# Attention with normed q and k, then an MLP: squares and sums by head, a k copy in two parts, one MLP copy on VectorE

## The chip, the cores and the metric

The kernel runs on one core of a Trainium2 chip. The metric is device time in microseconds (us) of one execution. Engines: TensorE (PE; its weight loads are PEld), VectorE (DVE), ScalarE (ACT), GpSimd (POOL) and SyncE (SP), which issues DMAs. Each engine runs its own instructions in order; semaphores order them across engines. Each kernel has several timed runs and one profiled execution.

## What is computed

q, k and v have the shape (8, 12, 448, 64): batches, heads, sequence, head dimension. Cut to what matters:

```python
def rmsnorm(x, g):
    return x / np.sqrt(np.mean(x * x, axis=-1, keepdims=True) + 1e-6) * g
q_n, k_n = rmsnorm(q, g_q), rmsnorm(k, g_k)
scores = np.matmul(q_n, k_n.transpose(0, 1, 3, 2)) / np.sqrt(64)
attn = softmax(scores)
x = np.matmul(attn, v)                 # then (3584, 768): heads side by side
h = x @ w_in                           # (3584, 2048)
g = np.maximum(h, 0) + alpha * np.minimum(h, 0)
out = g @ w_out                        # (3584, 768), float32
```

## The kernel before

**Tiling.** The 12 heads of a batch are taken four at a time, so there are 3 groups per batch and 24 groups in all, numbered y. A group's q (or k) is one tile `nat` of 128 partitions by 2 heads, 7 sequence parts and 64 values: 64 partitions for one half of the heads and 64 for the other, with 2 heads of each half beside each other. Its 448 keys are 7 key tiles j of 64.

**A group's preparation.** `load_qk` loads q and k. `square` writes squares in float32 to `sq` (line 148, GpSimd; q of group 1 on ScalarE). `reduce` sums them over the 64 values to `ss` (line 154, VectorE, one instruction of 128 x 896 for q and one for k). `root` takes logarithm and exponential on ScalarE (lines 165 and 166) to get the reciprocal root `rr`. `scale` multiplies `nat` by `rr` to `qs` in float16 (line 171; VectorE for groups 0 to 2 and q of group 3, GpSimd from then on). TensorE transposes the 7 parts into PSUM (`tps`), and VectorE copies these to SBUF as `qT` and `kT`, multiplying k by the gains. Group 0 does it in parts of its own (`part_...`), group 1 in `turn_one` (q: line 256, k: line 258), groups 2 to 6 in `turn` (lines 298 and 300), later groups by a transposing DMA. `follow` is a tiny GpSimd copy `mark` (line 244) that holds GpSimd back until VectorE's scaling is done.

**Attention.** `score(y, j)` makes the scores of one key tile (line 315) in one of two PSUM buffers `sc`; `soft` takes the exponential on ScalarE into `expT` (line 329). `den` and `attv` sum the exponentials and multiply them by v (line 344); `log` and `invert` (lines 361 and 366) give the reciprocal of the sums, with which VectorE writes `xT` (lines 393 and 395).

**MLP.** `up(b, ft)` makes one of 16 blocks `hT` of h for a batch (line 410). The MLP copy `ah` = alpha times h is ScalarE's (line 447); of ft = 2 and 3 of the first batch it is VectorE's (line 441), whose maxima are put off until ft = 4. `tensor_max` on VectorE writes `gT` (line 449). `down` multiplies by w_out (line 459), copies to `osb` (line 471) and stores (line 479).

**Order.** It is written by hand. The 168 key tiles are cut into bursts n (0: tiles 0 and 1 of group 0, 3: tile 6 of group 0 and tile 0 of group 1, 4: tiles 1 and 2 of group 1, and so on). `bursts`, `dens`, `avs`, `turns` and `gaps` say what stands in each burst; `post` (filled by `after`) holds what is appended behind a burst, `mid[1] = 1` and `mid[4] = 2` put a group's root and scaling ahead of the burst's last exponential. `reduce` of group 2 stands behind burst 3, that of group 3 (G = 3) behind a later burst, `square` two bursts before it. `spin` makes matrix products on idle data between the first bursts (line 488).

```python
    def root(y, nms="qk"):
        ...
        nc.scalar.activation(out=rr, in_=ss, func=AF.Ln, scale=1.0 / D, bias=epsb[:, 0:1])
        nc.scalar.activation(out=rr, in_=rr, func=AF.Exp, scale=-0.5)
```

Of the kernel before, what the change touches and what calls it, by code (L numbers as in the profile page):

```python
# [11 lines left out]
AF = mybir.ActivationFunctionType  # L12
ALU = mybir.AluOpType
AXIS_X = mybir.AxisListType.X
# [7 lines left out]
def kernel(  # L22
# [12 lines left out]
    nc = tc.nc  # L35

    B, H, S, D = q.shape
    DM = H * D
    DF = moe_w_in.shape[1]
    J = S // 64  # L40
    HH = H // 2
    G = HH // 2
    KM = DM // 128
    NF = DF // 128
# [39 lines left out]
    alpha_sb = cols[:, :NF]  # L84
    gain = cst.tile([128, 1], FP32, name="gain", tag="gain")
# [7 lines left out]
    nat, sqs, qs, ss_t, rr_t, qkT, vt, xT = {}, {}, {}, {}, {}, {}, {}, {}  # L93
# [47 lines left out]
    def square(y, nm):  # L141
        src = nat[y, nm].rearrange("p h j d -> p (h j d)")
        sq = ld.tile([128, 2 * J, D], FP32, name="sq", tag="sq", bufs=4)
        sqf = sq.rearrange("p n d -> p (n d)")
        if (y, nm) == (1, "q"):
            nc.scalar.activation(out=sqf, in_=src, func=AF.Square)
        else:
            nc.gpsimd.tensor_mul(out=sqf, in0=src, in1=src)  # L148
        sqs[y, nm] = sq

    def reduce(y, nm):
        if nm == "q":
            ss_t[y] = ld.tile([128, 2, 2, J], FP32, name="ss", tag="ss", bufs=4)
        nc.vector.tensor_reduce(  # L154
            out=ss_t[y][:, "qk".index(nm)].rearrange("p h j -> p (h j)").unsqueeze(2),
            in_=sqs[y, nm], axis=AXIS_X, op=ALU.add,
        )

    def root(y, nms="qk"):
        n = len(nms)  # L160
# [85 lines left out]
    def turn_one(y, nm):  # L246
        t = psf.tile([128, 512], FP32, name="tps", tag="mm")
        tp = t[:, :S].bitcast(FP16).rearrange("p (j c) -> p j c", j=J)
        for j in range(J):
            nc.tensor.transpose(  # L250
                tp[:, j, :], qs[y, nm][:, j].rearrange("p h d -> p (h d)"), ident
            )
        t = att.tile([128, J, 2, 64], FP16, name=f"{nm}T", tag=f"{nm}T", bufs=4)
        o = t.rearrange("p j g c -> p j (g c)")
        if nm == "q":
            nc.vector.tensor_copy(out=o, in_=tp)
        else:
            nc.vector.tensor_scalar(
                out=o, in0=tp, scalar1=gain[:, 0:1], scalar2=None, op0=ALU.mult
            )  # L260
        qkT[y, nm] = t

    def turn_dma(y):
# [134 lines left out]
    def bank(name, spare):  # L398
        if spare:
            t = psa.tile([128, 2, 512], FP32, name=name + "a", tag="acc")  # L400
            return t[:, 0]
        return psf.tile([128, 512], FP32, name=name, tag="mm")
# [3 lines left out]
    def up_part(hT, b, ft, lo, hi):  # L406

        for i in range(lo, hi):
            for g in range(2):
                nc.tensor.matmul(  # L410
                    out=hT[:, :S],
                    lhsT=w_in_sb[:, g * G + i, ts(ft, 128)],
                    rhs=xT[b][:, g, i, :],
                    start=(i == 0 and g == 0),
                    stop=(i == G - 1 and g == 1),
                )
# [10 lines left out]
    held = []  # L427

    def up(b, ft, spare=False):
        if b == 0 and ft in begun:  # L430
            hT = begun[ft]

            for n in {2: (2, 3), 3: ()}.get(ft, (ft,)):
                up_part(begun[n], 0, n, G - 1, G)
        else:
            hT = bank("hT", spare)
            up_part(hT, b, ft, 0, G)
        ah = ffn.tile([128, S], FP16, name="ah", tag="ah", bufs=3)
        if b == 0 and ft in (2, 3):

            nc.vector.tensor_scalar(
                out=ah, in0=hT[:, :S], scalar1=alpha_sb[:, ft : ft + 1], scalar2=None,
                op0=ALU.mult,
            )
            held.append((hT, ah, ft))
            return
        nc.scalar.activation(out=ah, in_=hT[:, :S], func=AF.Copy, scale=alpha_sb[:, ft : ft + 1])  # L447
        for hT, ah, ft in [(hT, ah, ft)] + (held if b == 0 and ft == 4 else []):
            nc.vector.tensor_max(out=gT[:, ft, ds((b & 1) * S, S)], in0=hT[:, :S], in1=ah)  # L449

# [52 lines left out]
    while m < NG * J or steps:  # L503
        n = len(bursts)
# [20 lines left out]
        while len(bursts[n]) < limit and m < NG * J:  # L525
            y, j = divmod(m, J)
# [13 lines left out]
    def at(n, f, *a):  # L540
        prep.setdefault(max(int(n), 0), []).append((f, a))

    def after(n, f, *a):
        post.setdefault(max(int(n), 0), []).append((f, a))
# [9 lines left out]
    for y in range(G, NG):  # L554

        early = y < G + 2
        if early:
            n = turn_at[y - 1] + 1
        elif y == G + 2:
            n = den_at[G - 1]  # L560
        elif y == 2 * G:
            n = turn_at[y] - 4
        elif y % G == 1:
            n = den_at[y - 4] - 1
        elif y % G:
            n = den_at[y - G]
        else:
            n = av_at[y - 4]
        if y in (3 * G - 1, 3 * G):

            after(den_at[G] - (y < 3 * G), load_qk, y)
        else:
            at(n - (6 if early else 3 if y == 2 * G else 4 if y < 3 * G else 5), load_qk, y)
        for nm in "qk":
            if y != 2 * G:
                after(n - 2, square, y, nm)
            if early:
                after(n, reduce, y, nm)
            else:
                jobs.setdefault(n + (y == G + 2 and nm == "k"), []).append((reduce, (y, nm)))  # L580
        if y == 3 * G:
            after(n, *jobs[n].pop()[:1], y, "k")
        roots[n + 1 + (y in (G + 2, 3 * G))] = y
# [7 lines left out]
    for b in range(B):  # L591
        ups = [(UP / 3 if b == 0 and ft < 4 else UP, up, (b, ft)) for ft in range(NF)]
        odd = b % 2
        new = [
            (DOWN, down, (b - odd, t, oh))
            for t in (range(3, J) if odd else range(3)) for oh in range(2)
        ]
        if b == 0:
            new.sort(key=lambda u: u[2][2])
        tail = len(new) if b == B - 1 else 4 if b == 0 else 2 if odd else 1  # L600
        periods.append((ups, carry, new[:tail]))
        carry = new[tail:]
# [65 lines left out]
    for n, g in enumerate((g_q, g_k)):  # L668
        for h in range(2):
            nc.gpsimd.dma_start(  # L670
                out=rows[NF + n : NF + n + 1, ds(64 * h, 64)], in_=g.unsqueeze(0)
# [12 lines left out]
    for h in range(2):  # L684
# [8 lines left out]
    part_scale("k", lo, K0, nc.vector)  # L693
    part_root("k", hi)
    square(1, "q")
    nc.vector.tensor_copy(out=cols, in_=ct[:, : NF + 2])
    nc.vector.tensor_mul(
        out=gain, in0=cols[:, NF : NF + 1], in1=cols[:, NF + 1 : NF + 2]
# [6 lines left out]
    part_scale("k", hi, J - K0, nc.vector)  # L705
    follow(0, "k")
    square(1, "k")
    reduce(1, "q")
    square(2, "q")
    after(0, part_turn, "k", range(K0, J))  # L710
    after(0, part_copy, "k", hi, nc.vector)
    after(0, reduce, 1, "k")
    mid[1] = 1
    after(1, square, 2, "k")
    after(1, load_w_in, 0)
    for nm in "qk":
        after(3, reduce, 2, nm)
    after(5, load_w_in, 1)
    after(7, load_w_in, 2)
    after(8, load_w_in, 3)  # L720
# [7 lines left out]
    for n in range(NB):  # L728
# [6 lines left out]
        for t in first_tiles:  # L735
            if t == (0, J - 2):
                spin(1)
            elif t == (1, J - 3):
                spin(2, False)
            elif t == (1, J - 2):  # L740
                spin(1, False)
            elif t == (0, J - 1):
                turn_one(1, "q")
            elif t == (1, 0):
                turn_one(1, "k")
            elif t == (1, J - 1):
                turn(2)
            score(*t)
            if n == den_at[G - 1] - 1 and t == tiles[-1]:
                begin(0)  # L750
                begin(1)
            elif lead and t == tiles[0]:
                soft(*t)
                den(dens[n])
                attv(avs[n], 0, True, (log, invert))
            elif lead and t == tiles[1]:
                begin(2)
# [28 lines left out]
        if n in roots:  # L786
            y = roots[n]
# [41 lines left out]
        for k, (f, a) in enumerate(gaps[n]):  # L829
# [3 lines left out]
            else:  # L833
                f(*a, spare)
                done += 1
                if n in jobs and not (lead and done < 5):
                    g, c = jobs[n].pop(0)
# [3 lines left out]
                while late and done == late[0][0]:  # L841
                    _, g, c = late.pop(0)
# [43 lines left out]
```

## Time and profile before

| | |
|---|---|
| median of 6 runs | 430.32 us (429.41 to 431.14) |
| profiled execution's own time | 429.86 us |
| its span, first to last instruction | 427.7 us |
| mean granted TensorE clock | 0.995 |
| busy: PE, ACT, DVE, POOL | 97%, 65%, 49%, 40% |
| exponentials, line 329 | 168 of 1003 ns |
| reductions, line 154 | 46 of 1076 ns |
| GpSimd squares, line 148 | 45 of 1681 ns |

Times in the profile count from the span's start. The page shows busy time, the span in 40 slices, DMA queues, the chain of work that ended last, and the costliest groups of instructions. The timeline lists one engine's instructions by time; where like instructions follow each other they are one row, with their count behind an x. In brackets stands the time the engine sat idle before a row, and what ended it. "By stretches" gives the busy time in chosen stretches, the clock granted to TensorE (1.00 is full speed) and the DMA engines' share.

### The profile page before, as it was taken

The numbers are of one execution on the slowest core, as the hardware profiler recorded it, in microseconds if no ns is written. First come the engines' busy times: TensorE is split into PE (matmuls) and PEld (weight loads), VectorE is DVE, ScalarE is ACT, GpSimd is POOL, SyncE is SP. The second block draws the span as 40 slices with busy tenths as digits, with TensorE's granted clock in tenths as the row PEclk, the third lists the DMA queues.
The fourth block names the chain that finished last, engine by engine and source line by source line (L and its number), as shares of the span: only waits on it lengthen the run. The fifth ranks groups of instructions, "written<-read, shape, count | busy, mean of one in ns | idle before, by whom it ended". The sixth has DMA issues, their size and how long they took to land.

```text
span 427.7 us, 11526 instructions
## 1 busy us (share of the span) xinstructions
PE 416.6 (97%) x4975; PEld 216.9 (51%) x4975; DVE 207.9 (49%) x314; ACT 276.5 (65%) x385; POOL 172.5 (40%) x135
## 2 busy tenths in 40 slices
PE   8799999999999999999999999999999999999996
PEld 3334445544455555554555445544555445555564
DVE  4865954456544454545345463545453453243421
ACT  5898888778875685768576676767666577132200
POOL 6679994475467209360465408380253000000000
PEclk9989999999999999999999999999999999999999
DMA  8999999999389804986278823863083201211033
GB/s 203 255 234 189 194 202 209 195 188 227 66 147 162 220 12 83 193 152 141 41 120 189 190 67 80 171 138 95 21 149 74 62 1 21 57 38 37 20 74 76
DMA packets 68531, 53.39 MB, mean 125 GB/s; under 512 B 35568, under 2 KB 68480, under 8 KB 68480
## 3 DMA queue, kind: packets, MB, share of 16 engines
q1 hardware_dynamic: 53680, 39.73, 42.1%
q0 software_dynamic: 13984, 11.81, 18.9%
q10 hardware_dynamic: 816, 1.11, 1.0%
q8 instruction: 39, 0.64, 0.6%
q14 instruction: 12, 0.10, 0.1%
HBM read 45.62 MB, written 11.01 MB: 132 GB/s over the span
## 4 chain that ended last, share of the span: by engine, by line
PE 90%; ACT 5%; DVE 2%; POOL 1%; issue 1%; ACTq 1%; POOLq 0%
PE op L459 29%; PE hT L410 22%; PE hTa L410 11%; PE sc L315 8%; PE opa L459 6%; PE dn L344 5%; PE av L344 5%; ACT expT L329 3%; PE avb L344 2%; DVE osb L471 1%; ACTq L105 1%; PE tps L291 1%; PE spin L488 1%; PE hTb L410 1%; ACT ah L447 0%
## 5 line engine op out<-in xcount | busy, mean ns | idle before, releaser
L329 ACT ACTIVATE expT<-sc,expb 128x896 f16<-128x896 f32 x168 | 161.5, 1003 | 36.9 <-PE sc L315 36.1
L171 POOL TENSOR_TENSOR qs<-nat,rr 128x896 f16<-128x896 f32 x41 | 70.0, 1728 | 139.6 <-issue 93.2
L459 PE MATMUL op<-w_out_sb,gT 128*128 128x384 f16 (+1 forms) x752 | 126.3, 323 | 0.0
L459 PEld LDWEIGHTS <-gT 128*128 128x128 f16 x912 | 85.8, 98 | 64.6 <-issue 12.0
L410 PEld LDWEIGHTS <-w_in_sb 128*128 128x128 f16 x768 | 73.3, 98 | 72.4 <-issue 7.7
L410 PE MATMUL hT<-xT,w_in_sb 128*128 128x448 f16 x510 | 106.6, 353 | 0.0
L447 ACT ACTIVATE ah<-hT,cols 128x448 f16<-128x448 f32 x85 | 53.7, 633 | 45.2 <-PE hT L410 45.1
L148 POOL TENSOR_TENSOR sq<-nat 128x896 f32<-128x896 f32 x45 | 74.7, 1681 | 7.4 <-DMA nat<-in_q_dram 4.1
L449 DVE TENSOR_TENSOR gT<-hT,ah 128x448 f16<-128x448 f32 x85 | 52.8, 623 | 49.0 <-ACT ah L447 49.0
L471 DVE COPY osb<-op 128x384 f32<-128x384 f32 (+1 forms) x47 | 25.7, 548 | 88.0 <-PE op L459 88.0
L315 PE MATMUL sc<-qT,kT 64*32 64x448 f16 (+1 forms) x1092 | 53.7, 357 | 4.7 <-ACT expT L329 2.3
L410 PE MATMUL hTa<-xT,w_in_sb 128*128 128x448 f16 x246 | 53.2, 352 | 0.0
L154 DVE TENSOR_REDUCE ss<-sq 128x14 f32<-128x896 f32 x46 | 48.4, 1076 | 0.8 <-POOL sq L148 0.8
L447 ACT ACTIVATE ah<-hTa,cols 128x448 f16<-128x448 f32 x41 | 26.0, 634 | 31.4 <-PE hTa L410 31.4
L449 DVE TENSOR_TENSOR gT<-hTa,ah 128x448 f16<-128x448 f32 x41 | 25.6, 623 | 26.7 <-ACT ah L447 26.7
L315 PEld LDWEIGHTS <-kT 64*32 64x32 f16 (+1 forms) x1092 | 15.4, 93 | 36.8 <-issue 29.8
L459 PE MATMUL opa<-w_out_sb,gT 128*128 128x384 f16 x160 | 27.7, 326 | 0.0
L395 DVE TENSOR_TENSOR xT<-av,rden 128x896 f16<-128x896 f32 x16 | 17.5, 1091 | 19.7 <-PE av L344 16.7
L344 PEld LDWEIGHTS <-vt 64*32 64x32 f16 (+1 forms) x1260 | 18.9, 94 | 13.1 <-issue 2.1
L344 PE MATMUL dn<-expT,ones 64*32 64x448 f16 (+1 forms) x812 | 24.2, 350 | 0.9
L344 PE MATMUL av<-expT,vt 64*32 64x448 f16 (+1 forms) x812 | 24.1, 349 | 0.0
L361 ACT ACTIVATE rden<-dn 128x896 f32<-128x896 f32 x16 | 14.5, 906 | 7.3 <-PE dn L344 7.3
(59 smaller groups left out, 168.2 us busy)
## 6 DMA issues: line engine op xcount, KB each, us to landing
out_dram<-osb SPq DMA_DIRECT2D x109, 96.0 KB, 2.3
nat<-in_q_dram SPq DMA_DIRECT2D x46, 224.0 KB, 4.9
nat<-in_k_dram SPq DMA_DIRECT2D x46, 224.0 KB, 5.4
vt<-in_v_dram POOLq DMA_DIRECT2D x16, 336.0 KB, 8.2
w_in_sb<-in_moe_w_in_dram POOLq DMA_DIRECT2D x12, 256.0 KB, 7.0
w_out_sb<-in_moe_w_out_dram POOLq DMA_DIRECT2D x4, 768.0 KB, 10.9
nat<-in_q_dram ACTq DMA_DIRECT2D x2, 224.0 KB, 4.4
nat<-in_k_dram ACTq DMA_DIRECT2D x2, 224.0 KB, 5.4
```

What stands on the lines that cost most here:

```text
L148: nc.gpsimd.tensor_mul(out=sqf, in0=src, in1=src)
L154: nc.vector.tensor_reduce(out=ss_t[y][:, "qk".index(nm)].rearrange("p h j -> p (h j)").unsqueeze(2), in_=sqs[y, nm], axis=AXIS_X, op=ALU.add,)
L171: eng.tensor_mul(out=t.rearrange("p j h d -> p h j d"), in0=nat[y, nm], in1=rr_t[y][:, "qk".index(nm)].unsqueeze(3).broadcast_to((128, 2, ...
L315: nc.tensor.matmul(out=sc[ds(64 * g + m * c, m), par, :S].rearrange("p (j c) -> p j c", j=J), lhsT=kT[ds(64 * par, 64), j, g, ts(c, m)], r ...
L329: nc.scalar.activation(out=expT[y][:, j], in_=scs[y, j][:, :, :S], func=AF.Exp, scale=QK_SCALE, bias=expb[:, 0:1],)
L344: nc.tensor.matmul(out=accs[g][ds(m * h, m), :S], lhsT=weights(g, y, par, ts(c, m), j), rhs=expT[y][ds(64 * g, 64), j, par, :], start=(j = ...
L395: nc.vector.tensor_mul(out=x, in0=av[:, :, :S], in1=r)
L410: nc.tensor.matmul(out=hT[:, :S], lhsT=w_in_sb[:, g * G + i, ts(ft, 128)], rhs=xT[b][:, g, i, :], start=(i == 0 and g == 0), stop=(i == G ...
L447: nc.scalar.activation(out=ah, in_=hT[:, :S], func=AF.Copy, scale=alpha_sb[:, ft : ft + 1])
L449: nc.vector.tensor_max(out=gT[:, ft, ds((b & 1) * S, S)], in0=hT[:, :S], in1=ah)
L459: nc.tensor.matmul(out=ops[c][:, :PW], lhsT=gT[:, ft, ts(t, 128)], rhs=w_out_sb[:, ft, ds(oh * OH + c * PW, PW)], start=(ft == 0), stop=(f ...
L471: nc.vector.tensor_copy(out=o[:, ts(c, PW)], in_=ops[c][:, :PW])
```

## The change

Four edits. GpSimd's squares of q of group 2 and of k of group 3 become two instructions, one for each of the tile's two heads (448 columns each). The sums of these two are taken by head too: for q of group 2 the first head's sum is appended behind burst 0 (so it stands ahead of group 1's scaling on VectorE) and the second head's stays behind burst 3; for k of group 3 both stay where the one was. `turn_one` copies k of group 1 from PSUM in two instructions, of key tiles 0 and 1 and of tiles 2 to 6. And the MLP copy of ft = 12 (NF - 4) of the first batch goes from ScalarE to VectorE, its maximum directly behind it. All else, TensorE's and SyncE's orders included, stays as it is.

```diff
@@ square
-            nc.gpsimd.tensor_mul(out=sqf, in0=src, in1=src)
+            n = 2 if (y, nm) in ((2, "q"), (G, "k")) else 1
+            for h in range(n):
+                c = ts(h, 2 * J * D // n)
+                nc.gpsimd.tensor_mul(out=sqf[:, c], in0=src[:, c], in1=src[:, c])
@@ reduce
-    def reduce(y, nm):
-        if nm == "q":
+    def reduce(y, nm, heads=None):
+        if y not in ss_t:
             ss_t[y] = ld.tile([128, 2, 2, J], FP32, name="ss", tag="ss", bufs=4)
-        nc.vector.tensor_reduce(
-            out=ss_t[y][:, "qk".index(nm)].rearrange("p h j -> p (h j)").unsqueeze(2),
-            in_=sqs[y, nm], axis=AXIS_X, op=ALU.add,
-        )
+        o = ss_t[y][:, "qk".index(nm)].rearrange("p h j -> p (h j)").unsqueeze(2)
+        for c in [slice(0, 2 * J)] if heads is None else [ts(h, J) for h in heads]:
+            nc.vector.tensor_reduce(
+                out=o[:, c], in_=sqs[y, nm][:, c], axis=AXIS_X, op=ALU.add
+            )
@@ turn_one
-            nc.vector.tensor_scalar(
-                out=o, in0=tp, scalar1=gain[:, 0:1], scalar2=None, op0=ALU.mult
-            )
+            for c in (slice(0, 2), slice(2, J)):
+                nc.vector.tensor_scalar(
+                    out=o[:, c], in0=tp[:, c], scalar1=gain[:, 0:1], scalar2=None,
+                    op0=ALU.mult,
+                )
@@ up
-        if b == 0 and ft in (2, 3):
+        if b == 0 and ft in (2, 3, NF - 4):
             nc.vector.tensor_scalar(
                 out=ah, in0=hT[:, :S], scalar1=alpha_sb[:, ft : ft + 1], scalar2=None,
                 op0=ALU.mult,
             )
-            held.append((hT, ah, ft))
-            return
-        nc.scalar.activation(out=ah, in_=hT[:, :S], func=AF.Copy, scale=alpha_sb[:, ft : ft + 1])
+            if ft < 4:
+                held.append((hT, ah, ft))
+                return
+        else:
+            nc.scalar.activation(
+                out=ah, in_=hT[:, :S], func=AF.Copy, scale=alpha_sb[:, ft : ft + 1]
+            )
@@ the order of the groups' preparation
-                after(n, reduce, y, nm)
+                after(n, reduce, y, nm, (0, 1) if (y, nm) == (G, "k") else None)
@@ the order by hand
     after(0, reduce, 1, "k")
+    after(0, reduce, 2, "q", (0,))
     mid[1] = 1
     after(1, square, 2, "k")
     after(1, load_w_in, 0)
-    for nm in "qk":
-        after(3, reduce, 2, nm)
+    after(3, reduce, 2, "q", (1,))
+    after(3, reduce, 2, "k")
```

## The prediction

> **What bounds the kernel now.** I read the page's busy shares and its chain first, then busy time by stretches, then the timelines of the first 65 us engine by engine, since every edit lies there.
>
> ```profile
> PE 416.6 (97%) x4975; PEld 216.9 (51%) x4975; DVE 207.9 (49%) x314; ACT 276.5 (65%) x385; POOL 172.5 (40%) x135
> PE 90%; ACT 5%; DVE 2%; POOL 1%; issue 1%; ACTq 1%; POOLq 0%
> ```
>
> TensorE is the bound. By stretches of 40 us it is busy 39.85 or 40.00 of 40 from 65 us on, so what the head wins by 64 us reaches the end, and nothing later gives it back. The head is another matter. Its stretches of 3.41 us (columns: stretch, its length, TensorE busy with its count, granted clock, DMA share, GB/s):
>
> ```profile
> 10.30:13.71 3.41, 2.29 (x23) 1.00 1.09 265
> 13.71:17.12 3.41, 3.28 (x27) 1.00 1.22 241
> 17.12:20.54 3.42, 1.72 (x23) 1.00 1.19 252
> 20.54:23.95 3.41, 3.41 (x16) 0.50 1.13 252
> 23.95:27.36 3.41, 2.68 (x35) 1.00 1.22 239
> ```
>
> After a stretch that is busy to 0.50 the clock is at half for 3.41 us; after one busy to 0.67 (2.29 of 3.41) it is not. The timelines of VectorE, TensorE and ScalarE there (start, length, instruction, and in brackets the idle time before it and what ended it):
>
> ```profile
> 17.30 0.62 DVE L256 COPY qT<-tps 128x896 f16<-128x896 f16 x1
> 18.04 0.68 DVE L258 TENSOR_SCALAR kT<-tps,gain 128x896 f16<-128x896 f16 x1
> 18.64 2.07 DVE L154 TENSOR_REDUCE ss<-sq 128x14 f32<-128x896 f32 x2
> 18.78 0.57 PE L315 MATMUL sc<-qT,kT 64*64 64x448 f16 x8 [0.78 <-DVE kT L258]
> 20.59 1.86 PE L488 MATMUL spin<-gT 128*128 128x448 f32 x2
> 22.38 0.59 PE L315 MATMUL sc<-qT,kT 64*64 64x448 f16 x4
> 19.21 1.90 ACT L329 ACTIVATE expT<-sc,expb 128x896 f16<-128x896 f32 x2 [0.37 <-PE sc L315]
> 23.02 1.01 ACT L329 ACTIVATE expT<-sc,expb 128x896 f16<-128x896 f32 x1 [0.54 <-PE sc L315]
> 24.27 4.70 ACT L329 ACTIVATE expT<-sc,expb 128x896 f16<-128x896 f32 x5 [0.25 <-PE sc L315]
> ```
>
> Scores of group 1 wait 0.78 for the one copy of its k (L258), then ScalarE waits 0.37 for the scores. At half clock the spin takes 1.79 until the next scores at 22.38, where the same spin at 15.07 took 0.95, and ScalarE waits again, 0.54 and 0.25. From 24.27 to 33.92 the chain is mostly ScalarE's: exponentials, root, logarithm, inverse. TensorE has it from 33.96. So the head's price is ScalarE's three waits. The last place is at 57 us:
>
> ```profile
> 57.17 0.62 ACT L447 ACTIVATE ah<-hT,cols 128x448 f16<-128x448 f32 x1
> 57.69 1.00 ACT L329 ACTIVATE expT<-sc,expb 128x896 f16<-128x896 f32 x1
> 58.74 0.38 PE L315 MATMUL sc<-qT,kT 64*64 64x448 f16 x4 [0.31 <-ACT expT L329]
> 57.83 0.62 DVE L449 TENSOR_TENSOR gT<-hT,ah 128x448 f16<-128x448 f32 x1 [1.26 <-ACT ah L447]
> ```
>
> TensorE waits 0.31 for the exponential that stands behind the MLP copy of ft = 12.
>
> **The k copy in two parts.** One instruction of 0.68 becomes two, of 256 and 640 columns. This form's rows are 0.408 (384 columns), 0.486 (512) and 0.684 (896): 0.20 + 0.54 ns a column. So 0.34 and 0.55, overlapping by 0.08 as neighbours here do. The scores of key tiles 0 and 1 read only the first part, so they start at 18.44 instead of 18.78. ScalarE's exponentials before run to 18.84, so its next starts at 18.87: 0.34 won, and the 0.37 wait is gone. The second part ends at 18.85, 0.17 later than now; its first reader, tile 2, stood at 20.27 and moves to 19.93, so 1.08 cover it. Behind it on VectorE stand group 2's reductions.
>
> **Group 2's q by head.** They would end 0.17 later (20.88) while ScalarE comes to the root 0.34 earlier (21.01 to 20.67): a wait of 0.2. So half a reduction goes ahead, into VectorE's 0.64 of idle before 15.29. It costs 0.61 (the 448-column row of L194). GpSimd's two squares run from 11.85 to 15.16; the first half of the second is there at about 14.4, VectorE is free at 14.56, ends at 15.18, and the scaling of group 1 at 15.29 is not late. Afterwards one half reduction (18.77 to 19.38) and k's, which needs the square that ends at 19.33, end at 20.43. The root finds them done with 0.24 to spare. The price is on GpSimd: a second instruction. No row shows a half square; its extra lies between nothing and 0.19 (the `mark` copy, a whole small GpSimd instruction); I take 0.05, since two full squares follow each other with 1.64 between starts at a length of 1.68. Up to 0.13 hides ahead of 15.29. Above that VectorE's scaling might wait: at 29.52 a GpSimd scaling beside VectorE's own took 2.58 instead of 1.68, so these two forms can exclude each other. At worst 0.06.
>
> The page SBUF — State Buffer of the Trainium skill (section SBUF: two separate sides) says that a VectorE instruction with two SBUF inputs and a GpSimd one exclude each other for a whole instruction. The row at 29.52 agrees.
>
> **Group 3's k by head.** GpSimd's squares at 23.99 follow VectorE's scaling, which follows the root: 0.34 earlier, so they end at about 27.0, with the first half at 26.2. If ScalarE has won 1.28 by then it wants the root at 27.58. VectorE: q's reduction 25.2 to 26.3, the first half to 26.8, the second 27.02 to 27.63: 0.07 late. Undivided it would end at 28.10, 0.5 late. With 0.54 won (below) the root is wanted at 28.32, and both forms are in time. GpSimd then issues w_in loads (27.25 to 29.42, about 0.3 earlier) before scaling group 3's k; that scaling ended at 32.10, its transposes stand at 32.97, so 0.9 cover it, and as VectorE's scaling would now be ahead of it, it needn't take 2.58.
>
> **The clock.** The stretch 17.12 to 20.54 gains 0.34 of busy time: 2.06 of 3.42, share 0.60, between 0.50 (fell) and 0.67 (held). If it still falls at 20.54: the spin starts at 20.25, does 0.29 of its 0.95 at full clock and 0.66 in 1.32, ends at 21.86, 0.52 ahead of 22.38; ScalarE's exponentials at 23.02 and 24.27 come 0.52 to 0.54 earlier. Won: 0.54. If it holds: the two gaps vanish; start to start they cost 23.02 - 21.49 - 0.91 = 0.62 and 24.27 - 23.02 - 0.91 = 0.34. Won: 0.34 + 0.96 - 0.07 = 1.23.
>
> TensorE: Matmul & The Clock Gate of the Trainium skill (section Why this matters for your kernels) says that the clock falls after an idle gap of about 3 us. Here gaps of 0.78 and 0.92 were enough, so the measurement decides; by the page there would be no fall in either kernel and the sum would be 0.34 + 0.31.
>
> **The MLP copy of ft = 12.** ScalarE loses 0.62; the exponential behind it starts at 57.17 instead of 57.69 and ends at 58.18, and the scores that waited follow those at 58.05 directly, at 58.43: 0.31 won. VectorE gains an instruction of 0.67 (L441) into an idle of 1.26: hT is done at 56.85, copy to 57.52, maximum to 58.1 instead of 58.45, so the bank is free earlier. If VectorE were not idle, 0.67 would stand before that maximum.
>
> **The sum.** Against the profiled execution's 429.86 (span 427.7 and 2.16 around it): 0.54 + 0.31 = 0.85 if the clock falls, 1.23 + 0.31 = 1.54 if it holds. The reported time is a median of executions that differ by 1.7 us among themselves before, and that median, 430.32, is 0.46 above the profiled one. Where the clock's stretches lie may differ between executions; the share 0.60 is midway between held and fallen. So I take the middle, 1.2: 429.1. What a measurement of this kernel can tell from no change is about 0.2%, 0.86 us.
>
> **The rivals.** *The clock falls as before* (against: 0.34 more busy time; for: 0.60 is near 0.50): 430.32 - 0.85 = 429.5.
> *The gain is lost in part before 34 us.* GpSimd's part wins only 0.3, and if the scaling of group 3's k takes 2.58 again from 29.2 it ends at 31.8 against transposes wanted at about 31.7; executions that never fell win only 0.34. Then 0.34 + 0.31 = 0.65 or somewhat less: 429.8.
> *Slower: the clock falls at another place.* A stretch that would now be busy to 0.50 or less between 23.95 and 30.8 costs up to half of 3.41, 1.7, where TensorE is close behind the chain: 1.7 - 0.85 = 0.85 more, 431.2. The decision point is 1.7 busy in such a stretch. Against: 23.95 to 27.36 has 2.68, and the earlier exponentials only shorten its gap of 0.60.
> *It doesn't do what it says*: were scores of tile 0 held by the second part, they would start at 18.9, and 0.17 be lost in the head. In the changed program the wait on VectorE moves to tile 2's weights, which speaks against it; I count it in the second rival.
>
> **Numbers.** Forecast 0.48, clock falls 0.32, lost in part 0.13, slower 0.07. The first is faster by over 0.86 in 0.43, the second half the time (0.16), the third hardly (0.01): faster 0.60, same 0.33, slower 0.07. The range goes from the full 1.54 with some more, 428.4, to the third case with 0.5 of scatter, 430.3.
>
> **What would show it.** After: VectorE's first k part about 0.34 long, scores of group 1 near 18.44, no ScalarE wait there; a half reduction before 15.3; clock 1.00 from 20.5 to 24 (or 0.50 and the second case); the scores near 58 us without a wait on an exponential; TensorE's first down product near 62.7 instead of 63.88. Wrong: a wait of group 1's scaling on GpSimd, a root waiting for a reduction, or a half-clock stretch elsewhere.

## The result and the profile after

| | before | after |
|---|---|---|
| median | 429.88 us (44 executions, 429.40 to 431.14) | 429.30 us (20, 428.42 to 430.38) |
| ratio, after to before | | 0.9977, 95% interval 0.9970 to 0.9985 |
| profiled execution | 429.86, span 427.7 | 429.40, span 427.6 |
| ... to the end of the last matrix product | 423.87 | 423.23 |
| ... from there to the span's end | 3.80 | 4.39 |
| ... outside the span | 2.19 | 1.78 |

Faster by 0.23%, 0.98 us between the means that the ratio compares (430.09 and 429.12). Between the two medians it is 0.58, and 1.02 from the median that the prediction started from. The forecast was 429.1. But the last three rows say that the profiled pair gets there in a way that the prediction doesn't have: the head of the program wins 0.63, the end of the program loses 0.59, and 0.41 is won outside the span.

Executions of one kernel differ by how many stretches of half clock (3.41 us each) fall into the head, which the mean granted clock tells: about 1.00 for none, 0.996 for one, 0.992 for two. Times are therefore also compared at an equal number (medians of all timed executions, us):

| | none | one | two |
|---|---|---|---|
| before | 429.45 | 429.87 | 430.77 |
| after | 428.49 | 429.36 | 430.38 (one execution) |

So at an equal number of stretches the change wins 0.96, 0.51 and 0.39 us. The mix differs too. By their times 14 of the 44 executions of before have none, 14 one and 16 two; of the 20 after, 9 have none, 10 one and 1 two. The gain at an equal number, averaged with the shares of before, is 0.57 us, with those of after 0.64. The other 0.3 to 0.4 of the 0.98 us comes from executions with two such stretches having become rare.

The page of the changed kernel, busy line and chain (before: PE 416.6, ACT x385, DVE x314, POOL x135, chain ACT 5%):

```profile
PE 415.7 (97%) x4975; PEld 217.0 (51%) x4975; DVE 209.2 (49%) x318; ACT 276.2 (65%) x384; POOL 172.0 (40%) x137
...
PE 91%; ACT 3%; DVE 2%; issue 1%; POOL 1%; ACTq 1%; POOLq 0%
```

VectorE has four instructions more, GpSimd two more, ScalarE one less. TensorE is 0.9 less "busy" with as many products; products under half clock count as longer work. ScalarE's share of the chain went from 5% to 3%.

Stretches of 3.41 us in the changed kernel (columns as before: stretch, length, TensorE busy with its count, granted clock, DMA share, GB/s):

```profile
8.67:12.08 3.41, 1.91 (x20) 1.00 1.08 239
12.08:15.49 3.41, 3.35 (x15) 0.50 1.14 227
15.49:18.90 3.41, 3.41 (x30) 1.00 1.21 205
18.90:22.32 3.42, 2.12 (x19) 1.00 1.13 251
22.32:25.73 3.41, 2.95 (x33) 1.00 1.10 228
```

The boundaries lie 1.6 us earlier against the program than in the profiled execution of before. So the clock fell at 12.08, before the edited place, and held from 20.5 to 24. This puts the whole head behind 12 us about 0.9 later than in an execution at full clock; differences between rows still read well. The edited place on TensorE and ScalarE in this execution:

```profile
19.38 0.64 PE L323 MATMUL sc<-qT,kT 64*64 64x448 f16 x8 [0.44 <-DVE kT L265]
19.82 1.91 ACT L337 ACTIVATE expT<-sc,expb 128x896 f16<-128x896 f32 x2 [0.23 <-PE sc L323]
22.09 6.47 ACT L337 ACTIVATE expT<-sc,expb 128x896 f16<-128x896 f32 x7
28.73 0.32 ACT L170 ACTIVATE rr<-ss,epsb 128x28 f32<-128x28 f32 x1 [0.17 <-DVE ss L160]
```

The scores of group 1 wait 0.44 for k instead of 0.78: the 0.34 of the prediction. Seven exponentials run without a gap where before had gaps of 0.54 and 0.25. The root of group 3 now waits 0.17 for a sum. The MLP place:

```profile
57.93 0.57 PE L323 MATMUL sc<-qT,kT 64*64 64x448 f16 x8
58.43 0.95 PE L299 MATMUL tps<-ident,qs 128*128 128x128 f16 x14
56.90 0.68 DVE L449 TENSOR_SCALAR ah<-hT,cols 128x448 f16<-128x448 f32 x1 [0.46 <-PE hT L418]
63.25 0.98 PE L472 MATMUL op<-w_out_sb,gT 128*128 128x384 f16 x5
```

Eight scores follow each other, and the transposes come 0.50 after the first of them instead of 1.01 (58.05 to 59.06). The first down product stands at 63.25 instead of 63.88. The rows of before:

```profile
58.05 0.38 PE L315 MATMUL sc<-qT,kT 64*64 64x448 f16 x4
59.06 0.95 PE L291 MATMUL tps<-ident,qs 128*128 128x128 f16 x14
63.88 2.44 PE L459 MATMUL op<-w_out_sb,gT 128*128 128x384 f16 x14
```

Then the end of the program, which the prediction took to be the same. The DMA view from shortly before the last two stores' issue (from 424 us in before, from 423.5 in after): of its queues the row of q14 (packets, MB and share of the window), then the issues with size and us from issue to landing. q14 is a queue that loads instructions. First before, then after:

```profile
q14 instruction: 1, 0.01, 0.3%
issues: line engine op xcount, KB each, median us to landing
out_dram<-osb SPq DMA_DIRECT2D x1, 48.0 KB, 1.9
out_dram<-osb ACTq DMA_DIRECT2D x1, 48.0 KB, 2.1
```

```profile
q14 instruction: 1, 0.01, 0.9%
issues: line engine op xcount, KB each, median us to landing
out_dram<-osb SPq DMA_DIRECT2D x1, 48.0 KB, 2.6
out_dram<-osb ACTq DMA_DIRECT2D x1, 48.0 KB, 2.7
```

The same two stores take 0.6 to 0.7 longer to land. In both there is one load of instructions (8192 bytes). By its start in the trace it comes at 429.29 before, 1.6 behind the span's end, and at 424.81 after, in the middle of the last stores, issued at 423.66. Where this load falls is what the last experiment turns on.

### The profile page after: what moved, and what is told of

It reads as the page before. It is cut to its first block, busy times and chain, and to the rows that moved or that the text cites. A ratio compares the mean times of both kernels' runs of the same rounds, so it can differ in the third digit from the quotient of the medians.

```text
span 427.6 us, 11531 instructions
## 1 busy us (share of the span) xinstructions
PE 415.7 (97%) x4975; PEld 217.0 (51%) x4975; DVE 209.2 (49%) x318; ACT 276.2 (65%) x384; POOL 172.0 (40%) x137
## 4 chain that ended last, share of the span: by engine, by line
PE 91%; ACT 3%; DVE 2%; issue 1%; POOL 1%; ACTq 1%; POOLq 0%
PE op L472 29%; PE hT L418 22%; PE hTa L418 11%; PE sc L323 8%; PE opa L472 6%; PE dn L352 5%; PE av L352 5%; PE avb L352 2%; ACT expT L337 2%; DVE osb L484 1%; PE spin L501 1%; POOL sq L152 1%; ACTq L105 1%; PE tps L299 1%; PE hTb L418 1%
## 5 line engine op out<-in xcount | busy, mean ns | idle before, releaser
L152 POOL TENSOR_TENSOR sq<-nat 128x896 f32<-128x896 f32 (+1 forms) x47 | 74.9, 1617 | 7.7 <-DMA nat<-in_q_dram 7.6
L160 DVE TENSOR_REDUCE ss<-sq 128x14 f32<-128x896 f32 (+1 forms) x48 | 48.7, 1037 | 1.4 <-POOL sq L152 1.2
```

What stands on the lines that cost most here:

```text
L152: nc.gpsimd.tensor_mul(out=sqf[:, c], in0=src[:, c], in1=src[:, c])
L160: nc.vector.tensor_reduce(out=o[:, c], in_=sqs[y, nm][:, c], axis=AXIS_X, op=ALU.add)
```

## The experiments

Theory: the k copy and the MLP copy win time on the path of ScalarE and TensorE in the head, the sums by head keep the roots from giving it back, and the clock adds or takes some tenths. Rivals: one of the four edits does it all; the clock does it.

**Each of the two copies alone.** The first kernel is that of before with only the two-part copy in `turn_one`, the second with only `ft in (2, 3, NF - 4)` in `up`.

Expected of `kcopy_alone`:

> The kernel before, with the copy of group 1's k in two parts and nothing else. Theory (the head's waits add up): scores of group 1 start about 0.34 us earlier, but group 2's reductions end 0.17 later, so ScalarE's root waits about 0.2: 0.15 to 0.2 us won at equal clock, ratio about 0.9995; the share of executions without a half-clock stretch rises a little. Rival (only the clock matters): executions with the same granted clock take the same time as before, within 0.1 us. Rival (the copy alone brings all of the head): 0.35 us or more.

Measured: 429.45 median (428.96 to 430.63), ratio 0.9993 (0.9982 to 1.0005); with no half-clock stretch 429.00 against 429.45. Of these 0.45 only about 0.1 lies in the span (427.2 against 427.3); outside it the execution takes 1.81 instead of 2.13, see below. The timelines of TensorE and ScalarE, at full clock, show why the span wins so little:

```profile
18.47 0.83 PE L317 MATMUL sc<-qT,kT 64*64 64x448 f16 x8 [0.45 <-DVE kT L259]
18.90 1.90 ACT L331 ACTIVATE expT<-sc,expb 128x896 f16<-128x896 f32 x2
20.89 0.32 ACT L165 ACTIVATE rr<-ss,epsb 128x28 f32<-128x28 f32 x1
28.34 0.32 ACT L165 ACTIVATE rr<-ss,epsb 128x28 f32<-128x28 f32 x1 [0.50 <-DVE ss L154]
```

The 0.34 is won at 18.47, and then the root of group 2 stands at 20.89 instead of 20.67 and that of group 3 waits 0.50 for its sum. Without the sums by head ScalarE gives back what the k copy won.

Expected of `mlp_alone`:

> The kernel before, with the MLP copy of ft = 12 on VectorE and nothing else. Theory: 0.31 us won at any clock, ratio 0.9993, and TensorE's wait of 0.31 on an exponential near 58.7 us gone; nothing changes before 55 us, so the granted clocks occur as often as before. Rival (only the clock matters): no difference at equal clock. Rival (the wait moves to the next exponential): under 0.1 us won.

Measured: 429.94 (428.71 to 430.76), ratio 0.9992 (0.9980 to 1.0003). Six of its eleven executions had two half-clock stretches (clock 0.992) and a seventh, 429.62, stands between one and two (0.994), so the median says little; with none it took 428.71 and 429.00 (before 429.45), with one 429.14 and 429.27 (before 429.87). The place itself, TensorE's timeline:

```profile
58.13 0.57 PE L315 MATMUL sc<-qT,kT 64*64 64x448 f16 x8
58.64 0.95 PE L291 MATMUL tps<-ident,qs 128*128 128x128 f16 x14
```

0.51 instead of 1.01: this edit wins 0.5, with nothing else changed, and not 0.31.

**The sums by head taken away**, one at a time and both: in `square`, `n = 2 if (y, nm) in ((G, "k"),) else 1` or `((2, "q"),)`, with the reductions to match; `two_edits` is the kernel of before with both copies and nothing by head.

Expected of `no_q_by_head`:

> The changed kernel without squares and sums of q of group 2 by head. Theory: ScalarE's root of group 2 waits about 0.2 us for VectorE's reductions, so it is 0.2 us slower than the changed kernel at equal clock, ratio to the kernel before about 0.998. Rival (group 2's root has slack behind it): the same as the changed kernel.

Expected of `no_k_by_head`:

> The changed kernel without squares and sums of k of group 3 by head. Theory: where the clock doesn't fall, ScalarE's root of group 3 waits for a reduction that ends up to 0.5 us later, so the fastest executions are about 0.4 us slower than the changed kernel's 428.45; where the clock falls, no difference. Rival: no difference anywhere, the root has slack.

Expected of `two_edits`:

> The kernel before with the k copy in two parts and the MLP copy on VectorE, without squares and sums by head. Theory as it stands after the runs that left out one of these: they don't add at full clock, so the fastest executions are near 428.5 (429.0 of the copy alone less 0.5 of the MLP copy). Rival (the two by-head edits cover for each other): about 0.3 us slower, 428.8.

Measured: 428.54 (ratio 0.9968, 0.9957 to 0.9980), 428.51 (0.9970, 0.9957 to 0.9983) and 429.18 (0.9979, 0.9968 to 0.9990). With no half-clock stretch the medians are 428.37, 428.50 and 428.48, against 428.49 of the changed kernel. So by the time alone the sums by head bring nothing. By the timeline they do: without k by head the root of group 3 waits 0.50 again, ScalarE's row there:

```profile
28.15 0.32 ACT L170 ACTIVATE rr<-ss,epsb 128x28 f32<-128x28 f32 x1 [0.50 <-DVE ss L160]
```

Without q by head the root of group 2 comes 2.43 after the first scores of group 1 (18.90 and 21.33) instead of 2.24 (18.45 and 20.69 in the profile of the changed kernel at full clock, below). Something else had to take as much from the kernels that have them. At this point that was open.

**The clock held by idle products.** Idle 16-bit products in TensorE's waits ahead of scores (`fill`, on data that nobody reads): seven in the kernel of before, six in the changed one and in `two_edits` (one instead of two ahead of key tile 0 of group 1), and in a last kernel only two, ahead of key tile 2 of group 1.

```diff
+            fills = {(0, 0): 2, (1, 0): 2, (1, 2): 3}
+            if fills.get(t):
+                fill(fills[t])
             score(*t)
```

Expected of `before_filled`:

> The kernel before, with idle 16-bit matrix products (2, 2 and 3 of 128x448) in TensorE's three waits: ahead of the first scores of group 0, ahead of tile 0 of group 1, and ahead of tile 2 of group 1. They write a PSUM buffer that nothing reads. Theory (half-clock stretches follow stretches of 3.41 us that are busy to less than about 0.6): the 1.71 of 3.41 rises to about 2.6, no stretch falls, all executions stand near the kernel before's own fastest, 429.4 to 429.5, median ratio 0.999. Rival (the half clock isn't what costs): median as before, 429.88. Rival (the fills delay the scores): 429.8 or more at full clock.

Expected of `after_filled`:

> The changed kernel with the same fills (2, 1 and 3). Theory: no half-clock stretch in nearly all executions, all near the changed kernel's fastest, 428.4 to 428.5, ratio 0.9968 to the kernel before. Rival (the remaining spread has another cause): a median of 429.3 and three groups of times as in the changed kernel.

Expected of `two_edits_filled`:

> The k copy in two parts and the MLP copy on VectorE with the fills (2, 1 and 3), without squares and sums by head. Theory: no half-clock stretch, all executions near 428.5. If the by-head edits matter only while they cover for each other, 0.3 us above the filled changed kernel.

Expected of `after_filled_two`:

> The changed kernel with two idle products only, ahead of key tile 2 of group 1. If the stall of TensorE at the first hT comes with the filled wait itself (work on the path), it stays at some tenths of a us; if it comes with the number of added instructions, it is smaller than with seven, under 0.2. Without half-clock stretch 428.45 us if nothing is lost, 428.7 and more if the stall stays.

Measured: 430.23 (ratio 1.0008), 429.30 (0.9983), 428.92 (0.9979) and 428.77 (0.9974, 0.9960 to 0.9988). Most executions of the first three then have no half-clock stretch (9 of 12, 10 of 12, 9 of 10), yet they take 429.86 to 430.61, 428.69 to 430.12 and 428.59 to 429.53, in the median 0.4 to 0.8 more than the same kernels without the products at full clock. TensorE's timeline of the changed kernel with six products:

```profile
33.25 0.74 PE L418 MATMUL hT<-xT,w_in_sb 128*128 128x448 f16 x3
34.76 1.12 PE L418 MATMUL hT<-xT,w_in_sb 128*128 128x448 f16 x5 [0.78 <-issue]
```

A wait of 0.78 that nothing in the profile explains stands in the first MLP block, where the changed kernel has eight products in 1.69 without one. In the profile of `before_filled` it is 0.31, in that of `two_edits_filled` the eight products take 1.85. With two products it isn't there (1.69 again) and executions at full clock take 428.50 to 428.88; only six of ten are then at full clock. Holding the clock with six or seven products gives back what it wins; what the wait is, and whether it is all that these kernels lose, stays open.

**Both kernels once more**, for a profile of the changed kernel at full clock.

Expected of `before_again`:

> The kernel before once more, for a profile at full clock. By the times seen, an execution whose mean granted clock shows no half-clock stretch in the head should take about 429.4 us, one with a stretch about 429.85; down products should begin near 63.3 in the first case, near 63.9 in the second.

Expected of `after_again`:

> The changed kernel once more, for a profile at full clock. Without a half-clock stretch about 428.45 us and a first down product near 62.3; with one about 429.35 and 63.25. If the gain at equal clock came from the two places of the prediction, the head ends 0.9 to 1.0 us earlier than in the kernel before at the same clock.

Measured: 429.95 with one stretch at half clock, and 428.49 with none; first down products at 64.01 and 62.33. TensorE ends at 422.32 in the second, 1.68 earlier than in the first, but the time differs by 1.46 and the span by 1.1: the end of the program gives 0.57 back again. Its last stores:

```profile
q14 instruction: 1, 0.01, 0.6%
issues: line engine op xcount, KB each, median us to landing
out_dram<-osb SPq DMA_DIRECT2D x1, 48.0 KB, 2.5
out_dram<-osb ACTq DMA_DIRECT2D x1, 48.0 KB, 2.7
```

**The load of instructions at the end.** The theory then was that GpSimd's two added squares move this load. The kernel `fewer_gpsimd` is the changed one with the small identity copied by VectorE instead of built by GpSimd:

```diff
-    make_identity(nc, ident32)
...
     nc.vector.memset(gT[:, 0, :], 0.0)
+    nc.vector.tensor_copy(out=ident32, in_=ident[:32, :32])
```

Expected of `fewer_gpsimd`:

> The changed kernel with the small identity (32 x 32) copied by VectorE from the large one instead of built by GpSimd: GpSimd's stream loses a memset, a select and what belongs to them, VectorE's gains one copy at 1 us. In the profiles so far the last two stores land 1.87 and 2.15 us after their issue; in all profiles of kernels with both edits by head they take 2.54 to 2.78 and 2.72 to 2.96, and there a load of 8192 bytes on the instruction queue falls into them, which without these edits comes after the program's end; with one of the two edits it falls into GpSimd's last instructions and 0.2 is lost. Theory (GpSimd's stream, two instructions longer, reaches one load more): the load goes back behind the end, the last stores take 1.87 and 2.15 again, 1.22 follows the last landing, and an execution at full clock takes 427.9 to 428.0 instead of 428.46. Rival (VectorE's stream, or the time at which the stores fall): the last stores stay at 2.5 and 2.7 or more and the time at 428.4 to 428.5.

Measured: 428.18 median (427.90 to 428.62), ratio 0.9960 (0.9946 to 0.9973); 427.90, 427.94, 428.18 and 428.57 without a half-clock stretch and 428.62 with one (changed kernel 429.36). The ratio flatters it: of the nine executions of before beside it none was without such a stretch. Its two fastest have spans of 426.1; less the 3.78 behind the last product that its profile shows, TensorE ends at 422.3, as in `after_again`. So by this estimate what it wins over the changed kernel lies behind TensorE's work and not in GpSimd's shorter start. The issues from 423.2 us on; this answer has no line of q14:

```profile
issues: line engine op xcount, KB each, median us to landing
out_dram<-osb SPq DMA_DIRECT2D x1, 48.0 KB, 1.9
out_dram<-osb ACTq DMA_DIRECT2D x1, 48.0 KB, 2.1
```

The numbers are those of the theory; the engine is not. The load did not go back behind the end, it came earlier still, at 421.69, ahead of the last stores. The profiles side by side, without those of idle products, in the order of VectorE's recorded instructions (with its semaphore instructions; times from the trace, in us):

| kernel | VectorE | GpSimd | load starts, from the last product's end | last store, issue to landing | last product to span's end | outside the span |
|---|---|---|---|---|---|---|
| before | 445 | 239 | +5.42 | 2.15 | 3.80 | 2.19 |
| kcopy_alone | 446 | 239 | +4.94 | 2.17 | 3.82 | 1.82 |
| mlp_alone | 447 | 239 | +4.88 | 2.14 | 3.79 | 1.90 |
| two_edits | 448 | 239 | +4.46 | 2.17 | 3.83 | 1.77 |
| no_k_by_head, no_q_by_head | 449 | 240 | +4.33 | 2.15 | 4.02 | 1.78, 1.81 |
| after, after_again | 450 | 241 | +1.57 | 2.73 | 4.38 | 1.79 |
| fewer_gpsimd | 451 | 238 | -1.34 | 2.14 | 3.78 | 1.81 |

The load moves forward with each instruction more in VectorE's stream, and not with GpSimd's: the first four rows have the same GpSimd count, and the last has fewest and the earliest load. The kernels with idle products, whose stores fall at other times, agree: +5.64 with 445 VectorE instructions, +4.44 with 448, +1.56 and +1.60 with 450. With 449 VectorE's last drain starts 0.47 behind its last semaphore wait (0.11 in the others), 0.2 lost in all; the load's own packet comes 0.7 behind that drain, so it would be the asking for it that costs, which the trace doesn't show. With 450 it falls into the last stores, 0.57. With 445 it ends latest, nearly 2 us behind the span, and these executions (the kernel with fills, also 445, as well: 2.13) take some 0.33 more outside the span. That this is the load's doing is not shown: it ends 1.5 us behind the span in `mlp_alone`, which takes 1.90 outside, and 1.6 behind it in `kcopy_alone`, which takes 1.82. `fewer_gpsimd` itself changed both counts; that it is VectorE's which moves the load, the other rows tell.

What follows: the theory of the head stands for all four edits (the k copy needs the sums by head; what these would win without it no run shows). The clock has its part beside it. Two half-clock stretches (mean granted clock 0.992 or less) were recorded in 24 of 83 executions of before and in 6 of 11 of `mlp_alone`, but in 4 of 65 of the kernels that have the k copy in two parts and no idle products. By these counts it is that copy that makes them rare, and this would be the 0.3 to 0.4 us of the result that the comparison at an equal number leaves over. The sums by head look worthless in the time because the kernels that have both lose as much behind TensorE's work, where the load then falls. `fewer_gpsimd` keeps them, has the load elsewhere, and is the fastest version that ran, 0.4 under the changed kernel with no half-clock stretch (four executions) and 0.7 with one (a single one).

## Why the prediction was right, and where not

**The k copy** was right to the hundredth: the wait of scores fell from 0.78 to 0.44. In `fewer_gpsimd` the clock happened to fall at 20.45, nearly where it fell before (20.54), so its rows stand beside those of before. TensorE, then ScalarE:

```profile
18.44 0.84 PE L323 MATMUL sc<-qT,kT 64*64 64x448 f16 x8 [0.44 <-DVE kT L265]
17.83 2.96 ACT L337 ACTIVATE expT<-sc,expb 128x896 f16<-128x896 f32 x3
20.67 0.32 ACT L170 ACTIVATE rr<-ss,epsb 128x28 f32<-128x28 f32 x1
22.52 1.01 ACT L337 ACTIVATE expT<-sc,expb 128x896 f16<-128x896 f32 x1 [0.38 <-PE sc L323]
23.89 4.73 ACT L337 ACTIVATE expT<-sc,expb 128x896 f16<-128x896 f32 x5 [0.37 <-PE sc L323]
```

Scores at 18.44 and root at 20.67 are as worked out, and ScalarE's wait of 0.37 is gone: the three exponentials from 17.83 on run without a gap. One slip in the working: by the prediction's own numbers the second part ends at 18.85 and the one copy at 18.72, so the split costs 0.13 and not 0.17; in `kcopy_alone` the reductions behind it start 0.15 later (18.79 against 18.64). For the case in which the clock falls, the exponentials of 23.02 and 24.27 were put 0.52 to 0.54 earlier. They came 0.50 and 0.38 earlier, and the second gap grew from 0.25 to 0.37. The clock came back 0.09 earlier only (23.86 against 23.95), so the scores ahead of that exponential, now 0.51 earlier, ran at half clock to their end. TensorE in before, then in `fewer_gpsimd`:

```profile
23.76 0.46 PE L315 MATMUL sc<-qT,kT 64*64 64x448 f16 x4
23.25 0.59 PE L323 MATMUL sc<-qT,kT 64*64 64x448 f16 x4
```

Worth 0.34 at the first MLP product (33.94 against 34.28) where 0.54 was forecast.

**The clock held**: at full clock the first MLP product stands at 33.23 (`after_again`), 1.05 ahead of the profiled execution of before; 1.23 was forecast. The root of group 3 waits 0.18 where 0.07 was expected, which is 0.11 of the 0.18 that is missing; three squares, two of them halves, take 3.46 on GpSimd where two whole ones took 3.31, so a second instruction costs 0.15 and not 0.05. ScalarE's row in `after_again`:

```profile
27.81 0.32 ACT L170 ACTIVATE rr<-ss,epsb 128x28 f32<-128x28 f32 x1 [0.18 <-DVE ss L160]
```

**The sums by head** were costed rightly: 0.2 without the half sum of q, 0.5 without k's; measured 0.2 (20.89 against 20.67) and 0.50.

**The MLP copy** was mis-sized, 0.31 for 0.51. The wait was counted and not what its end allows: eight scores in a row take 0.57 where four and four took 0.38 each, with the starts 0.69 apart. The prediction put the second four behind the end of the first (58.43); its own row at 18.78, eight in 0.57, says that they start sooner.

**Two errors that cancel.** The head was put too high by 0.18 or 0.20 and the MLP copy too low by 0.20, so the sums of both cases come out at the first down product, 63.88 before. In `after_again`, where the clock holds, it comes 1.55 earlier (1.54 was forecast); in `fewer_gpsimd`, where it falls, 0.84 earlier (0.85). That they meet to the hundredth is luck.

```profile
62.33 2.76 PE L472 MATMUL op<-w_out_sb,gT 128*128 128x384 f16 x16
63.04 1.14 PE L472 MATMUL op<-w_out_sb,gT 128*128 128x384 f16 x6
```

**Nothing later gives it back** is the step that failed. It was read off TensorE's busy shares, which end with TensorE. Behind its last product the stores grew by 0.57, and outside the span 0.41 went away in the profiled pair. The two nearly cancel, and the forecast started from the median of six executions, 430.32, where 44 give 429.88. So that the total came out close to the forecast is in part luck. At full clock the account is: TensorE ends about 1.2 earlier (span of before 427.3, less its 3.80, against 422.32), 0.57 is lost in the stores, 0.34 won outside the span: 0.95, and the runs show 0.96.

**The case "lost in part"** gave 0.65 for executions in which the clock never fell. They won 0.96. The rule used there was that such executions win the two waits alone, 0.34 and 0.31. From the ends of TensorE's work at full clock (423.35 with the k copy alone, 422.93 with the MLP copy too, 422.32 with the sums by head) the MLP copy brings 0.42 (the head of that profile is 0.08 later) and the sums by head 0.61; for the k copy alone 0.15 is left. GpSimd's scaling of group 3's k, 2.58 before, took 1.79 in `after_again`, so at full clock that part of this rival did not come; in `fewer_gpsimd` it took 2.50. That the edits need each other was in the prediction's parts, but not in this rival's sum. No profile of before at full clock was had, so its own waits there are not known.

**Clock and busy share.** The stretch ahead of 20.5 was to be busy 2.06 of 3.42, a share of 0.60, placed between 0.50 (fell) and 0.67 (held). Where a stretch lay nearly there, it came out at 2.22 to 2.24. The runs don't give a threshold. Stretches before a boundary in `fewer_gpsimd` and in `no_k_by_head`, each with the stretch behind it:

```profile
17.04:20.45 3.41, 2.22 (x25) 1.00 1.25 258
20.45:23.86 3.41, 3.41 (x13) 0.50 1.14 231
```

```profile
17.25:20.66 3.41, 2.24 (x24) 1.00 1.26 245
20.66:24.07 3.41, 3.06 (x29) 1.00 1.08 247
```

After 2.22 the clock fell and after 2.24 it held, while 2.12 held in the changed kernel's profile. After 1.69 to 1.91 it fell each time. Something besides the busy share decides; what, is open. The direction was right: with the copy's added busy time fewer stretches fall (4 of 65 executions with two, as counted above), and with idle products in the waits, which add busy time, most executions have none. Taking the middle between the two cases was right as a hedge: both occur.

## What to carry to other kernels

A gain in the head is followed through to the end of the last store, and to what lies outside the span, before it is booked: one instruction more or less on an engine far from the bound can move an instruction load into the last transfers, and here that was worth as much as an edit. When two versions should differ by the timeline and don't by the clock, compare the ends of their programs. And a wait of an engine is worth more than its length where its end lets two groups of work run together.

## What the runs showed of the hardware that was not expected

An engine's instructions are loaded in blocks, and a block's load can show: where one of 8192 bytes on an instruction queue fell into the last two stores of 48 KB, the later one landed 0.5 to 0.8 us later (2.67 to 2.96 us from issue to landing instead of 2.13 to 2.17). That is so in all four profiles with 450 VectorE instructions and in none of the others, and 0.2 were lost where the load's place was at VectorE's last drain. The Trainium skill (Runtime: NRT & Kernel Launch, section Instruction fetch mechanics) says that engines refill in blocks of 16 KiB on queues of their own, mostly hidden. The loads of one instruction queue here are 16384 bytes and agree; those of the other, q14, the one that moved with VectorE's count among them, were 8192, and at the end of the program not hidden.

The stretches of the granted clock are 3.41 us long in every profile and lie differently against the program in each execution, by 1.6 us between the two profiles compared above. Whether none, one or two stretches fall to half clock moves single executions by 0.4 to 1.0 us a stretch (table above), as much as the change is worth. The Trainium skill (TensorE: Matmul & The Clock Gate, section What's actually happening) says of the window that it runs freely, 3413 ns long; the runs agree.
